# Gathers behind the turned expert, a spread cut into chunks, and an earlier end of the sort: a DeltaNet block with a grouped mixture of experts

## The chip, the cores and the metric

The kernel runs on one core of a Trainium2 chip. TensorE (matmuls), VectorE, ScalarE, GpSimd and SyncE work side by side, each through its own queue in order, and wait for each other through semaphores; sixteen DMA engines move the data. The metric is the device time of one execution in microseconds (us).

## The reference

Two blocks follow each other. The first is a DeltaNet attention over 4 batches, 8 heads, 768 positions and 48 features per head; the keys are normalised first:

```
for t in range(S):
    y[:, :, t] = einsum('bhd,bhde->bhe', q[:, :, t], state)
    v_old = einsum('bhde,bhd->bhe', state, kt)
    state = state + bt * einsum('bhd,bhe->bhde', kt, vt - v_old)
```

Its output, laid out as 3072 tokens of 384 features, is the input x of the second block. That is a mixture of 16 experts in 4 groups. A token takes the group with the largest logit, then the expert with the largest logit inside this group; its result is the product of both softmax weights with `relu(x @ w1) @ w2` of that expert (384 to 1024 to 384).

## The kernel before

**Attention.** The sequence is cut into 24 chunks of 32 positions; one chunk of all batches and heads is a period of the loop over `u` (L672). Four chunks form a group (`RG = 4`). For each group `inverse(g)` (L268) builds on VectorE the inverse of 32x32 triangular matrices, 256 of them at a time, in some 90 dependent steps; its result is turned into `mt` (L372, one buffer) and then spread into `mtb` (L378): for each parity `a`, ScalarE copies `mt` times a mask of the parity. Before the change the first chunk's rows of both parities are spread first (two copies of 128x256), and the other three chunks' rows follow in one copy of 128x768 for each parity. `advance(u)` (L403) runs the recurrence: `a_ps` (L415), its copy `f` (L419), `w_ps` from `mtb` and `f` (L432), its copy `w` (L435), the state `s_ps` (L442) and its two copies into `s_bd` (L448), and the output `o_ps`, copied to `x` (L465). `mask` (L263) and `scale` (L396) prepare operands for it on VectorE. `gram` (L229) makes the products for a chunk ten periods ahead. `logits(u)` (L475) turns a finished chunk, copies it to `xt` (L486) and makes the router's logits.

**The order** is written out by hand: long tasks (`inverse`, `route`) are generators that are pushed forward between the recurrence's steps, either by `work(n)`, which hands out a share of VectorE's time, or by `allow(X)`, which releases a task held at the name X (`ACT_STEP`, `PE_STEP`, `SORT`, `NEXT`, ...). Each engine's queue follows this order.

**Routing.** `route(r)` (L495) takes the logits of a group of chunks: groups 0 to 4 hold four chunks each, 5 and 6 hold two each. It finds each token's expert and place in the expert's list. For `early` groups part of this runs on GpSimd and yields for whole periods; otherwise all of it is on VectorE. For each chunk a 128x256 matrix `at` (L583, two buffers) is compared out, and four matmul instructions sort the chunk's token numbers into `s_sort` (L590). `found` is the copy of the sorted lists (L734); `by_place` (L130) writes the lists of source rows, target rows and gates.

**Experts.** They run in order of their loads, with 224, 232, 220, ... 168 slots (`SLOTS`), the first one expert 0 fixed. For each: `hidden` (L833) makes `h_ps` with three PSUM buffers and `hid` by a ReLU on ScalarE (L842); `second` (L852) makes `y_ps` in three blocks with two buffers and copies them to `yt` (L860). In fp32 each matmul stands as two instructions, so each of the two products is 48 of them. The result is turned (`part_out`, L891), passed through DRAM, weighed (L905) and scattered by GpSimd (L867). Weights are loaded two experts ahead (L163, L170) by SyncE. The rows of experts 2 to 15 are gathered in quarters: `take_quarters` (L807) issues 6 or 7 indirect DMAs (L811) on GpSimd into `xq` (two buffers), and `cross_in` (L817) turns them into `xt` (L819). At the start of expert `e`, `fetch(e + 2)` calls the gathers; `cross_in(e + 1)` stands behind the first block of `second` of expert `e`, and VectorE reaches it directly behind `part_out(e - 1)`. GpSimd's order in this stage is the planner's, the other engines' is the program's.

The rows of experts 0 and 1 are gathered whole and turned by `turn_in` (L799), through PSUM tile `t_ps` with one buffer.

Of the kernel before, what the change touches and what calls it, by code (L numbers as in the profile page):

```python
# [8 lines left out]
F32 = mybir.dt.float32  # L9
I32 = mybir.dt.int32  # L10
AX = mybir.AxisListType
ALU = mybir.AluOpType
ACT = mybir.ActivationFunctionType
# [3 lines left out]
RG = 4  # L17
SHARE = 0.64
LEAD = 10
FIXED, TILE = 1, 128  # L20
LAST = 8
SLOTS = [224] * FIXED + [232, 220, 214, 208, 204, 202, 200, 198, 194, 190, 186, 184, 180, 174, 168]
ACT_STEP, PE_STEP, SOON, NEXT, TURN = "ScalarE", "TensorE", "end of the period", "next period", "its turn"
SORT, ROOTS, FACTOR = "sorting", "roots made", "factor made"


# [39 lines left out]
def deltanet_then_moe(  # L66
# [107 lines left out]
    with ExitStack() as first:  # L174
# [93 lines left out]
        def inverse(g):  # L268
# [105 lines left out]
            yield C * C  # L374
            turned_over.add(g)

            def spread(rows, a):
                nc.scalar.activation(mtb[:, rows, a], mt.rearrange("p i r -> p r i")[:, rows], ACT.Copy,  # L378
                                     scale=cut["parity"][:, a:a + 1])

            rest = slice(0, RG * H)
            yield ACT_STEP
            for a in range(2):
                spread(slice(0, H), a)
            mts[g] = mtb
            rest = slice(H, RG * H)
            for a in range(2):
                yield ACT_STEP
                spread(rest, a)
            mts[g] = mtb  # L390

        def scale(u):

# [101 lines left out]
        def route(r):  # L495
# [8 lines left out]
                               bufs=3)[:, 0:n]  # L504

            L5 = 1 + G
            early = n == RG
            lg = lg_.pop(r)[:, 0:n].rearrange("p n (s e) -> p n s e", s=L5)
            best, hot5, tie = small("best", [L5]), small("hot5", [L5, EG]), small("tie", [L5])
            sx = small("sx", [L5, EG])  # L510
# [68 lines left out]
            else:  # L579
                yield 128  # L580
            for g, u in enumerate(us):
                at = wk.tile([128, T, TILE], F32, tag="at", name=f"at{u}")
                (nc.gpsimd if early else nc.vector).tensor_scalar(  # L583
                    at.rearrange("p t i -> p (t i)"), cut["places"], place[:, u:u + 1], None,
                    op0=ALU.is_equal)
                if r < NGR - 2 and u == u0:
                    yield NEXT
                yield SORT
                for t in range(T):
                    nc.tensor.matmul(s_sort[:, t * 3 * NE:(t + 1) * 3 * NE], lhsT=at[:, t],  # L590
                                     rhs=mine[:, g].rearrange("p c e -> p (c e)"),
                                     start=False, stop=True, skip_group_check=True)
# [42 lines left out]
        with tc.manual_schedule(engines={mybir.EngineType.PE, mybir.EngineType.DVE,  # L635
                                         mybir.EngineType.Activation, mybir.EngineType.Pool,
                                         mybir.EngineType.SP}):
            nc.scalar.activation(rooted, cut["tiny"], ACT.Exp)
            homes = [None, s_ps[:, 0:2], s_ps[:, 2:4]]
            first_grams = ([(u, (0,)) for u in range(RG)] + [(u, (0, 1)) for u in range(RG, 2 * RG)]  # L640
                           + [(u, (1,)) for u in range(RG)])
            for i, (u, parts) in enumerate(first_grams):
                gram(u, homes[i % len(homes)], parts)
                for late, loads in bursts.get(i, ()):
                    nc.scalar.activation(late[:, 0:1], cut["tiny"], ACT.Copy)
                    for load in loads:
                        load()
            start(inverse(0), 1)
            work(22)
            for _ in range(6):  # L650
                work(12)
            scale(0)
            nc.gpsimd.memset(acc[:, 0], 0.0)
            nc.gpsimd.tensor_copy(what[:, :, 0:2], cut["ids"].rearrange("p (u c) -> p u c", c=2))
            ahead = advance(0)
            next(ahead)
            for u in range(2 * RG, LEAD):
                gram(u, homes[u % len(homes)])
            start(inverse(1), 0.95)
            made = 0  # L660
            while 0 not in mts:
                work(4)
                if 1 not in vhs and 0 in turned_over:
                    mask(0)
                    scale(1)
                allow(ACT_STEP)
                made += 1
                if made == LAST:
                    allow(ROOTS)
            allow(FACTOR)  # L670
            ahead_of = {u: [u + LEAD] if u + LEAD < NCH else [] for u in range(NCH + 1)}
            for u in range(NCH + 1):  # L672
                step = advance(u) if u < NCH else iter([None] * 4)
                turned = logits(u - 1) if u else iter([None] * 2)
                if u:
                    next(step)
                else:
                    step = ahead
                allow(FACTOR)
                allow(NEXT)  # L680
                allow(TURN)
                r = group_of.get(u - 2)
                if r is not None and group_of.get(u - 1) != r and r < NGR - 2:
                    start(route(r), 0.25)
                next(turned)
                work(10)
                allow(SORT)
                next(step)
                for v in ahead_of[u]:
                    gram(v)  # L690
                if ahead_of[u]:
                    next(step)
                    next(turned)
                else:
                    next(turned)
                allow(PE_STEP)
                allow(ACT_STEP)
                work(9)
                if not ahead_of[u]:
                    next(step)  # L700
                next(step)
                work(14)
                allow(ACT_STEP)
                allow(ROOTS)
                r = group_of.get(u - 1)
                if r is not None and group_of.get(u) != r and r >= NGR - 2:
                    start(route(r), 0.6 if r == NGR - 2 else 1)
                allow(SOON)
                if u % RG == RG - 3 and u // RG + 2 < NGR:
                    start(inverse(u // RG + 2), SHARE)  # L710
                work(12)
                if u + 1 < NCH:
                    mask(u + 1)
                if u + 2 < NCH:
                    scale(u + 2)
                if u + NB < NCH:
                    load_kq(u + NB)
                if u + NV < NCH:
                    load_kv(u + NV)
                if u < NCH:  # L720
                    nc.sync.dma_start(out=x_dram[u * 128:(u + 1) * 128], in_=xs[u])
                if pieces and u + LEAD >= NCH:
                    pieces.pop(0)()
            while behind:
                work(2)
                allow(PE_STEP)
                allow(ACT_STEP)
                allow(SOON)
                allow(NEXT)
                allow(SORT)  # L730

            n_ps = ps.tile([128, NE], F32, tag="s", name="n_ps")
            nc.tensor.matmul(n_ps, lhsT=ones, rhs=acc[:, NCH], start=True, stop=True)
            nc.vector.tensor_copy(found.rearrange("p t c e -> p (t c e)"), s_sort)  # L734
            by_place(found[:, :, :, 0:FIXED], slice(0, FIXED))
            nc.vector.tensor_copy(last, n_ps)


            key, rank = cp.tile([128, NE], F32, name="key"), cp.tile([128, NE], F32, name="rank")
            nc.vector.scalar_tensor_tensor(key, in0=last, scalar=16.0, in1=cut["tie"], op0=ALU.mult,  # L740
                                           op1=ALU.add)
            like = [128, NE, NE]
            nc.vector.tensor_tensor(table, key[:, None, :].to_broadcast(like),
                                    key[:, :, None].to_broadcast(like), op=ALU.is_gt)
            nc.vector.tensor_reduce(rank, table, axis=AX.X, op=ALU.add)
            nc.vector.tensor_tensor(table, rank[:, None, :].to_broadcast(like),
                                    cut["expert"][:, :, None].to_broadcast(like), op=ALU.is_equal)
# [48 lines left out]
                in_offset=bass.IndirectOffsetOnAxis(ap=rows[0:P, t:t + 1], axis=0))  # L796
        return xg

    def turn_in(xg, xt, i, P):  # L799

        t_ps = ps.tile([128, DC, P], F32, tag="t", name="t_ps", bufs=1)
        for j in range(DC):
            nc.tensor.transpose(out=t_ps[:, j], in_=xg[0:P, i, j * 128:(j + 1) * 128],
                                identity=ident[0:P, 0:P])
# [1 line left out]

    def take_quarters(rows, R):  # L807

        xq = mp.tile([128, T * TILE // BL, DB], F32, tag="xq", name="xq", bufs=2)
        for g in range(-(-R // BL)):  # L810
            nc.gpsimd.indirect_dma_start(  # L811
                out=xq[:, g, :], out_offset=None,
# [118 lines left out]
    with tc.manual_schedule(engines={mybir.EngineType.PE, mybir.EngineType.DVE, mybir.EngineType.SP,  # L931
                                     mybir.EngineType.Activation}):
        for i in range(T):
            turn_in(ready[0], xts[0], i, tiles_of[0][i])
        placed = sort_experts(mp)
        for e in range(FIXED, 2):
            load(e, fetch(e))
# [137 lines left out]
```

## Time and profile before

| what | value |
|---|---|
| median of 3 runs | 545.43 us (545.0 to 546.75) |
| the profiled execution's own time | 545.04 us |
| its span, first to last instruction | 543.1 us |
| TensorE busy | 475.2 us (87%) |
| VectorE busy | 243.7 us (45%) |
| GpSimd busy | 201.7 us (37%) |
| ScalarE busy | 185.6 us (34%) |
| mean granted TensorE clock | 0.963 |

Busy shares are means over two very different stages: the attention until about 231 us, and the experts from 247 us on. A granted clock of 1.00 stands for the upper of TensorE's two levels, 0.50 for the lower. Matmul rows show when TensorE's queue handed them out, with modelled ends; when their result was seen shows in the row of the engine that waited for them. GpSimd's spans are rough.

### The profile page before, as it was taken

The numbers are of one execution on the slowest core, as the hardware profiler recorded it, in microseconds if no ns is written. First come the engines' busy times: TensorE is split into PE (matmuls) and PEld (weight loads), VectorE is DVE, ScalarE is ACT, GpSimd is POOL, SyncE is SP. The second block draws the span as 40 slices with busy tenths as digits, with TensorE's granted clock in tenths as the row PEclk, the third lists the DMA queues.
The fourth block names the chain that finished last, engine by engine and source line by source line (L and its number), as shares of the span: only waits on it lengthen the run. The fifth ranks groups of instructions, "written<-read, shape, count | busy, mean of one in ns | idle before, by whom it ended". The sixth has DMA issues, their size and how long they took to land.

```text
span 543.1 us, 18129 instructions
## 1 busy us (share of the span) xinstructions
PE 475.2 (87%) x7814; PEld 437.7 (81%) x7814; DVE 243.7 (45%) x800; ACT 185.6 (34%) x381; POOL 201.7 (37%) x305
## 2 busy tenths in 40 slices
PE   3348999999999999958943999999999999999993
PEld 3336877888887788848932999899999999999993
DVE  3999999999999952255110101110111111011110
ACT  3226576765857666411001111111111111121220
POOL 0040302627246143231572155345555445451131
PEclk9999999999999999976985999999999999999997
DMA  5771535444315543015852586776899788888720
GB/s 169 268 254 53 167 138 159 145 145 149 113 67 162 160 153 110 33 32 141 273 181 59 179 275 207 260 219 214 287 301 288 245 271 289 254 270 292 274 84 21
DMA packets 57331, 99.94 MB, mean 184 GB/s; under 512 B 18973, under 2 KB 41431, under 8 KB 57249
## 3 DMA queue, kind: packets, MB, share of 16 engines
q1 hardware_dynamic: 51329, 88.76, 50.4%
q0 software_dynamic: 5920, 10.00, 6.1%
q8 instruction: 63, 1.03, 0.8%
q14 instruction: 19, 0.16, 0.1%
HBM read 84.61 MB, written 14.27 MB: 182 GB/s over the span
## 4 chain that ended last, share of the span: by engine, by line
PE 59%; ACT 12%; DMA 10%; DVE 5%; issue 5%; another core or an unknown queue 4%; SPq 3%; POOL 1%; ACTq 0%; POOLq 0%; DVEq 0%
PE h_ps L839 17%; PE y_ps L858 16%; DMA out_dram<-yo,to_i 5%; ACT s_bd L448 5%; PE w_ps L432 5%; ACT mtb L378 4%; PE s_ps L442 4%; PE l_ps L490 2%; PE g_ps L246 2%; PE o_ps L424 2%; PE a_ps L415 2%; DMA yr<-y_dram 2%; SPq L899 2%; PE s_ps L590 2%
## 5 line engine op out<-in xcount | busy, mean ns | idle before, releaser
L839 PE MATMUL h_ps<-xt,w 128*128 128x224 f32 (+15 forms) x768 | 137.6, 339 | 17.0 <-ACT hid L842 12.8
L839 PEld LDWEIGHTS h_ps<-xt,w 128*128 128x128 f32 x768 | 132.7, 195 | 19.5 <-ACT hid L842 13.8
L858 PE MATMUL y_ps<-hid,w 128*128 128x224 f32 (+15 forms) x768 | 133.0, 332 | 2.5 <-ACT yt L860 2.5
L858 PEld LDWEIGHTS y_ps<-hid,w 128*128 128x128 f32 x768 | 128.8, 190 | 3.7 <-ACT yt L860 3.5
L811 POOL DMA_INDIRECT xq<-x_dram,from_q x92 | 87.7, 954 | 40.0 <-issue 25.6
L905 DVE TENSOR_SCALAR yo<-yr,gate 128x384 f32<-128x384 f32 (+14 forms) x28 | 11.2, 418 | 169.8 <-DMA yr<-y_dram 139.7
L842 ACT ACTIVATE hid<-h_ps 128x448 f32<-128x448 f32 (+15 forms) x64 | 31.9, 502 | 129.1 <-PE h_ps L839 95.8
L867 POOL DMA_INDIRECT out_dram<-yo,to_i x32 | 34.0, 1062 | 85.1 <-DVE yo L905 69.9
L860 ACT ACTIVATE yt<-y_ps 128x224 f32<-128x224 f32 (+15 forms) x48 | 15.8, 336 | 120.4 <-PE y_ps L858 103.6
L355 DVE TENSOR_TENSOR t<-m 128x81 f32<-128x81 f32 (+13 forms) x156 | 51.7, 331 | 0.2
L361 DVE TENSOR_TENSOR m<-m,t 128x81 f32<-128x81 f32 (+13 forms) x156 | 51.7, 332 | 0.0
L448 ACT ACTIVATE s_bd<-s_ps 48x768 f32<-48x768 f32 x46 | 37.0, 804 | 10.4 <-PE s_ps L442 9.8
L338 DVE SCALAR_TENSOR_TENSOR m<-m 128x29 f32<-128x29 f32 (+27 forms) x174 | 40.2, 234 | 0.4
L891 DVE STREAM_TRANSPOSE yq<-yt 128x672 f32<-128x672 f32 (+2 forms) x14 | 11.9, 853 | 51.3 <-ACT yt L860 51.3
L432 PE MATMUL w_ps<-f,mtb 64*64 64x48 f32 x768 | 28.0, 224 | 3.8 <-ACT mtb L378 2.9
L583 POOL TENSOR_SCALAR at<-con,place 128x256 f32<-128x256 f32 x20 | 20.5, 1029 | 28.0 <-PE s_ps L590 27.8
L246 PE MATMUL g_ps<-kqt 48*32 48x64 f32 (+1 forms) x1216 | 18.1, 240 | 14.3 <-issue 9.6
L432 PEld LDWEIGHTS w_ps<-f,mtb 64*64 64x64 f32 x768 | 25.0, 138 | 6.5 <-ACT mtb L378 3.2
L415 PEld LDWEIGHTS a_ps<-s_bd,kqt 128*32 128x32 f32 x736 | 15.3, 111 | 16.3 <-ACT s_bd L448 8.2
L378 ACT ACTIVATE mtb<-mt,con 128x256 f32<-128x256 f32 (+1 forms) x24 | 28.2, 1202 | 0.7 <-DVE mt L372 0.6
L529 POOL TENSOR_TENSOR acc<-acc,hots 128x16 f32<-128x16 f32 x20 | 7.2, 361 | 55.2 <-DVE hots L527 54.0
L246 PEld LDWEIGHTS g_ps<-kqt 48*32 48x32 f32 x1216 | 14.5, 118 | 16.2 <-issue 10.9
(141 smaller groups left out, 572.9 us busy)
## 6 DMA issues: line engine op xcount, KB each, us to landing
w<-in_w_dram SPq DMA_DIRECT2D x29, 1536.0 KB
kv<-in_kv_dram SPq DMA_DIRECT2D x24, 448.0 KB
kqt<-in_kq_dram SPq DMA_DIRECT2D x20, 512.0 KB
x_dram<-x SPq DMA_DIRECT2D x24, 192.0 KB
w<-in_w_dram SPq DMA_DIRECT2D x24, 128.0 KB
y_dram<-yq SPq DMA_DIRECT2D x36, 84.0 KB
yr<-y_dram SPq DMA_DIRECT2D x14, 192.0 KB
kqt<-in_kq_dram SPq DMA_DIRECT2D x8, 256.0 KB
```

The costliest lines, as they stand in the source:

```text
L246: nc.tensor.matmul(g_out[quads[b], hh * NP + j, of], lhsT=kqt[rows, 0, j, quads[b]], rhs=kqt[rows, of, j, quads[b]], start=True, stop=True ...
L338: nc.vector.scalar_tensor_tensor(row, in0=m[:, j, 0:j], scalar=m[:, i, j:j + 1], in1=row, op0=ALU.mult, op1=ALU.add)
L355: nc.vector.tensor_tensor(tv, m[:, j + 2:, j:j + 1].to_broadcast([128, n, j]), m[:, j:j + 1, 0:j].to_broadcast([128, n, j]), op=ALU.mult)
L361: nc.vector.tensor_tensor(below, below, tv, op=ALU.add)
L378: nc.scalar.activation(mtb[:, rows, a], mt.rearrange("p i r -> p r i")[:, rows], ACT.Copy, scale=cut["parity"][:, a:a + 1])
L432: nc.tensor.matmul(w_ps[b, h], lhsT=mt[b, uu * H + (h % 2) * NP + h // 2], rhs=f[b, h], start=True, stop=True, skip_group_check=True)
L448: nc.scalar.activation(s_bd[rows, :, :, hh, :], s_at[rows, :, :, hh * D:(hh + 1) * D], ACT.Copy)
L811: nc.gpsimd.indirect_dma_start(out=xq[:, g, :], out_offset=None, in_=x_dram[:, :].rearrange("n (q c) -> (n q) c", q=4), in_offset=bass.Ind ...
L839: nc.tensor.matmul(h_ps[:, k], lhsT=w1[:, j, (f + k) * 128:(f + k + 1) * 128], rhs=xt[:, j, 0:R], start=(j == 0), stop=(j == DC - 1), skip ...
L842: nc.scalar.activation(hid[:, f:f + 2], h_ps, ACT.Relu)
L858: nc.tensor.matmul(y_ps, lhsT=w2[:, f, j * 128:(j + 1) * 128], rhs=hid[:, f], start=(f == 0), stop=(f == FC - 1))
L867: put = nc.gpsimd.indirect_dma_start(out=out[:, :], out_offset=bass.IndirectOffsetOnAxis(ap=to[0:P, i:i + 1], axis=0), in_=yo[0:P, :], in_ ...
```

## The change

1. `xq` has one buffer instead of two. A gather for the next expert then has to wait for the `cross_in` that reads the expert in front.
2. The spread of `mt` is eight copies of 128x256, a pair for each chunk, instead of two of 128x256 and two of 128x768. The first pair stays where it was; the other three pairs are released by a new name `SPREAD`, one copy behind `f` and one behind `xt` in each of the periods 1, 2, ... The very first copy is moved to VectorE.
3. Group 4 of the routing (the last one of four chunks) no longer counts as `early`, so that VectorE does its work; `at` has four buffers instead of two; `SORT` is allowed a second time in the last periods.
4. The lists of expert 0 are written from the PSUM sums directly, ahead of the copy to `found`, and the two turns of its rows go through two PSUM tiles.

```diff
+SPREAD = "spread"
...
-            def spread(rows, a):
-                nc.scalar.activation(mtb[:, rows, a], mt.rearrange("p i r -> p r i")[:, rows], ACT.Copy,
-                                     scale=cut["parity"][:, a:a + 1])
-
-            rest = slice(0, RG * H)
+            def spread(uu, a):
+                rows = slice(uu * H, (uu + 1) * H)
+                from_, by = mt.rearrange("p i r -> p r i")[:, rows], cut["parity"][:, a:a + 1]
+                if g == uu == a == 0:
+                    nc.vector.tensor_scalar(mtb[:, rows, a], from_, by, None, op0=ALU.mult)
+                else:
+                    nc.scalar.activation(mtb[:, rows, a], from_, ACT.Copy, scale=by)
+
             yield ACT_STEP
             for a in range(2):
-                spread(slice(0, H), a)
+                spread(0, a)
             mts[g] = mtb
-            rest = slice(H, RG * H)
-            for a in range(2):
-                yield ACT_STEP
-                spread(rest, a)
-            mts[g] = mtb
+            for uu in range(1, RG):
+                for a in range(2):
+                    yield SPREAD
+                    spread(uu, a)
...
-            early = n == RG
+            early = r < NGR - 2
...
-                at = wk.tile([128, T, TILE], F32, tag="at", name=f"at{u}")
+                at = wk.tile([128, T, TILE], F32, tag="at", name=f"at{u}", bufs=4)
...
+                if u:
+                    allow(SPREAD)
                 r = group_of.get(u - 2)
                 if r is not None and group_of.get(u - 1) != r and r < NGR - 2:
                     start(route(r), 0.25)
                 next(turned)
+                if u:
+                    allow(SPREAD)
...
                 allow(PE_STEP)
                 allow(ACT_STEP)
+                if u == 0:
+                    for _ in range(2):
+                        allow(SPREAD)
+                if u + 2 >= NCH:
+                    allow(SORT)
...
+            by_place(s_sort.rearrange("p (t c e) -> p t c e", t=T, c=3)[:, :, :, 0:FIXED],
+                     slice(0, FIXED))
             nc.vector.tensor_copy(found.rearrange("p t c e -> p (t c e)"), s_sort)
-            by_place(found[:, :, :, 0:FIXED], slice(0, FIXED))
...
-    def turn_in(xg, xt, i, P):
+    def turn_in(xg, xt, i, P, tag="t"):
-        t_ps = ps.tile([128, DC, P], F32, tag="t", name="t_ps", bufs=1)
+        t_ps = ps.tile([128, DC, P], F32, tag=tag, name="t_ps", bufs=1 if tag == "t" else None)
...
-        xq = mp.tile([128, T * TILE // BL, DB], F32, tag="xq", name="xq", bufs=2)
+        xq = mp.tile([128, T * TILE // BL, DB], F32, tag="xq", name="xq", bufs=1)
...
-            turn_in(ready[0], xts[0], i, tiles_of[0][i])
+            turn_in(ready[0], xts[0], i, tiles_of[0][i], "to"[i])
```

## Rows read from the trace of the kernel before

**Rows 1.** The page: shares of the chain that ended last, by engine

```profile
PE 59%; ACT 12%; DMA 10%; DVE 5%; issue 5%; another core or an unknown queue 4%; SPq 3%; POOL 1%; ACTq 0%; POOLq 0%; DVEq 0%
```

**Rows 2.** Stretches: length, busy us of PE, PEld, DVE, ACT, POOL, granted clock, DMA

```profile
40.00:195.70 155.70, 148.16 (x4318) 124.78 (x4320) 152.84 (x546) 103.67 (x188) 53.45 (x118) 1.00 0.41 132
...
247.40:259.70 12.30, 12.30 (x51) 11.75 (x51) 6.39 (x17) 1.63 (x3) 2.07 (x2) 0.75 0.73 172
...
270.30:298.80 28.50, 12.03 (x51) 10.36 (x50) 2.43 (x4) 1.82 (x5) 15.13 (x17) 0.70 0.39 117
...
396.50:526.50 130.00, 130.00 (x825) 129.95 (x824) 19.39 (x34) 25.09 (x60) 55.43 (x63) 1.00 0.79 262
```

**Rows 3.** Timeline of TensorE's matmuls: start, length, line, shapes, idle before

```profile
267.11 3.21 PE L858 MATMUL y_ps<-hid,w 128*128 128x224 f32 x16
270.15 6.63 PE L839 MATMUL h_ps<-xt,w 128*128 128x232 f32 x33
...
294.51 4.24 PE L839 MATMUL h_ps<-xt,w 128*128 128x232 f32 x12 [12.76 <-ACT hid L842]
...
307.99 9.08 PE L839 MATMUL h_ps<-xt,w 128*128 128x220 f32 x48
316.91 6.11 PE L858 MATMUL y_ps<-hid,w 128*128 128x220 f32 x32
323.99 3.24 PE L858 MATMUL y_ps<-hid,w 128*128 128x220 f32 x16 [0.97 <-ACT yt L860]
```

**Rows 4.** Timeline of ScalarE beside them

```profile
275.55 0.36 ACT L860 ACTIVATE yt<-y_ps 128x224 f32<-128x224 f32 x1 [8.15 <-PE h_ps L839]
293.90 1.46 ACT L842 ACTIVATE hid<-h_ps 128x464 f32<-128x464 f32 x3 [18.00 <-remote]
...
323.58 0.60 ACT L860 ACTIVATE yt<-y_ps 128x220 f32<-128x220 f32 x2 [5.93 <-PE y_ps L858]
```

**Rows 5.** Timeline of GpSimd: two unbroken runs of indirect DMAs, first and last

```profile
261.27 0.95 POOL L811 DMA_INDIRECT xq<-x_dram,from_q  x1 [6.83 <-DVE from_q L830]
...
286.33 0.94 POOL L811 DMA_INDIRECT xq<-x_dram,from_q  x1 [0.30 <-issue]
...
289.40 0.97 POOL L867 DMA_INDIRECT out_dram<-yo,to_i  x1 [0.30 <-issue]
...
310.67 1.00 POOL L811 DMA_INDIRECT xq<-x_dram,from_q  x1 [0.85 <-DVE xt L819]
...
318.24 0.94 POOL L811 DMA_INDIRECT xq<-x_dram,from_q  x1 [0.30 <-issue]
...
321.60 1.04 POOL L867 DMA_INDIRECT out_dram<-yo,to_i  x1 [0.31 <-issue]
```

**Rows 6.** Timeline of VectorE: expert 2's rows are turned

```profile
276.74 0.84 DVE L819 STREAM_TRANSPOSE xt<-xq 128x672 f32<-128x672 f32 x1
```

**Rows 7.** Stretches from one copy `w` to the next, columns as in the second group

```profile
102.58:111.22 8.64, 8.22 (x253) 6.87 (x257) 8.57 (x35) 7.10 (x12) 3.65 (x4) 1.00 0.51 169
...
119.86:127.78 7.92, 7.92 (x252) 6.85 (x257) 7.88 (x32) 4.51 (x9) 4.37 (x14) 1.00 0.48 165
```

**Rows 8.** ScalarE's groups by shape: the spread, count, busy us, mean ns

```profile
L378 ACT ACTIVATE mtb<-mt,con 128x768 f32<-128x768 f32 x12 | 19.9, 1662 | 0.0
...
L378 ACT ACTIVATE mtb<-mt,con 128x256 f32<-128x256 f32 x12 | 8.3, 741 | 0.6 <-DVE mt L372 0.6
```

**Rows 9.** Timeline around the last group's inverse

```profile
194.47 1.25 DVE L372 STREAM_TRANSPOSE mt<-m 128x1024 f32<-128x1024 f32 x1
...
199.57 1.35 ACT L378 ACTIVATE mtb<-mt,con 128x256 f32<-128x256 f32 x2
```

**Rows 10.** Timeline between attention and experts

```profile
240.18 0.26 DVE L734 COPY found<-s_ps 128x96 f32<-128x96 f32 x1 [1.28 <-PE s_ps L590]
...
246.11 0.74 PE L803 MATMUL t_ps<-con,xg 96*128 96x96 f32 x3 [0.65 <-DVE xt L805]
```

## The prediction

> **What bounds the kernel now.** I read first the chain that ended last, then stretches of the span, then timelines of the stretches that stood out. The chain goes to TensorE for 59% [rows 1], but as a mean over two stages. By stretches, the late experts are bound by TensorE alone: busy 130.0 of 130.0 us at full clock [rows 2]. There only fewer matmul instructions could help, and the change takes none away. In the attention TensorE is busy 148.16 of 155.70 us and VectorE 152.84 [rows 2]: both are nearly full, so a gain on one is soon capped by the other. What sticks out is the stretch of expert 1: TensorE busy 12.03 of 28.50 us [rows 2].
>
> In its timeline the second product of expert 0 is handed out until 267.11 + 3.21 = 270.32, and `hidden` of expert 1 starts, fills its three PSUM buffers, and stops at 276.78 [rows 3]. ScalarE is what should empty them. It reads the third block of `y_ps` at 275.55, though the matmuls were handed out 5.2 us before, and its first `hid` stands at 293.90, behind 18.00 us that end with something the trace can't name [rows 4]. TensorE resumes in full only at 294.51 [rows 3]. GpSimd issues indirect DMAs in one unbroken run from 261.27 to 290.37, 23 of them, 21 being gathers of experts 2, 3 and 4 [rows 5]. Two buffers let experts 2 and 3 go at once, and `cross_in` of expert 2 at 276.74 [rows 6] frees the buffer for expert 4 before the run is through. The stall ends 3.5 us after the run does.
>
> One stage later is the counterexample. A run of 9 (7 gathers, 2 scatters) lasts from 310.67 to 322.64 [rows 5]. `hidden` of expert 2, beside it, takes 9.08 us for 48 instructions without an idle time, so ScalarE was on time. Only the first two blocks of `second` were seen late, at 323.58, and that cost TensorE 0.97 us [rows 3, 4]. My reading: while GpSimd issues indirect DMAs without a break, signals from TensorE to ScalarE come through for about the first 9 us, and after that only when the run is over. With 9 in a row nearly nothing is lost, with 23 nearly all that lies behind the first nine.
>
> **One buffer for the gathers.** The instructions stay the same; a wait is added in front of each expert's gathers. The first run is then expert 2's 7 gathers alone, 7 x 1.25 = 8.8 us by the spacing (310.67 to 318.24 is six steps, 1.26 each [rows 5]), so 261.3 to about 270. Expert 3's have to wait for `cross_in` of expert 2, which VectorE reaches near the start of `hidden` of expert 1: some 2 to 4 us of pause. The next run is 7 gathers and 2 scatters, which has the length of the good one. So `hidden` of expert 1 should go at the pace of expert 2's: 9.08 x 232/220 = 9.58 us. It was done at 294.51 + 4.24 = 298.75 [rows 3]. Gone are 298.75 - 270.32 - 9.58 = 18.85 us. Against this I set one lateness as at 323.99, 1.0. **Net 17.9.** The bounds: if the pause doesn't clear what the first run delayed, 3 to 12 us of the stall remain (3.5 is how long it took to clear at 290.37; 12 is a run of 16 in place of 23: (16 - 7) x 1.3); at best all 18.85 go.
>
> Behind the added wait on GpSimd stand the scatters and the rest of its queue. For these nothing on TensorE's path waits soon: an expert's gathers have until its own `cross_in`, one expert's time further on. A late expert has two products of some 7.5 us, about 15 us in all, and its gathers take 6 x 1.26 = 7.6 us to issue, leaving about 7 for landing. I price this at 0 in the forecast; its cover being gone is the last rival.
>
> **The spread.** The two copies of 128x768 cost ScalarE 1.66 us each, those of 128x256 0.74 [rows 8]; the six new ones take 4.4 us a group in place of 3.3. A period with the long copy lasts 8.64 us, the period behind the spread 7.92 [rows 7]: 0.72 us for each of two periods. ScalarE's copies `f` and `x` stand behind the long ones, and TensorE's next step behind those. For groups 1 to 3 this makes six times 0.72, **4.3 us**; the other groups I count at nothing, the least sure part of this term. A short copy of 0.74 lies in the time in which ScalarE waits for TensorE anyway; where it doesn't fit whole I allow 0.05 for each of 18 pairs, 0.9 in all. So 3.4, from 1 (pairs that cost 0.2) to 5 (all groups gain). The cap is VectorE: the last group's `mt` is turned at 194.47 + 1.25 = 195.72 and read at 199.57 [rows 9], a lead of 3.85 us. TensorE can catch up no more than this, less some 0.4 for the copy put on VectorE. Both give **3.3**. That first copy on VectorE runs beside ScalarE's second one of the pair: nothing by itself.
>
> **Sort and start of the experts.** More buffers for `at` and the earlier `SORT` move matmul instructions of the sort ahead; their number stays. The lists written before `found` spare its 0.26 us on the way to the first gathers; the second PSUM tile spares the turn 0.65 us of waiting [rows 10], of which I take 0.4, since the copy behind it still has to be made. The sort's end I take at 0.25 gained, against 0.4 for the work put into full periods (group 4's routing on VectorE). **Net 0.5**, from -1 to +1.5.
>
> **The clock.** From 247.4 to 259.7 TensorE's granted level is 0.75 in the mean [rows 2], so half of these 12.3 us at the lower level: the first expert starts slow, after a transition in which TensorE did little. If the work starts 3.8 us earlier but the rise stays where it is, 3.8 us more of it run at half speed: 1.9 lost. If the rise moves with the work, 0. **I take 0.9**, the middle, since no row shows which.
>
> Sum: 17.9 + 3.3 + 0.5 - 0.9 = 20.8. From the profiled time of 545.04, which is 0.4 below the median shown, **524.3 us**.
>
> **Rivals.**
>
> *A part of the stall stays.* For: I don't know what the signals wait on, and a lateness could carry over from a run of 7 to one of 9 behind a pause of only 2 to 4 us, when clearing took 3.5 us in both rows. Against: 9 in a row did almost no harm. Remaining 3 to 12 us give 528 to 536.
>
> *The stall stays whole, the gathers being not its cause.* For: the first 18.00 us wait is put down to no engine, and the stretch is also one where the weights of expert 2 are loaded. Against: the DMA share there, 0.39, is half that of the late experts, 0.79, which have no such stall [rows 2]. Time: 545.04 - 3.3 - 0.5 + 0.9, about 542. The Trainium skill ("SBUF — State Buffer", section "SBUF: two separate sides") says that engines and DMAs reach SBUF by disjoint ports, so that neither slows the other. By that rule gathers would leave ScalarE alone and the time would be this rival's. The trace agrees with it in that `hidden` of expert 2 is undisturbed beside a run; it disagrees if the late blocks at 323.58 hang on that run.
>
> *No change that can be told:* the stall stays and the attention's gain is used up by VectorE: within 0.3%, 1.6 us, which is about what a measurement of this kernel can tell from none.
>
> *Slower: gathers come too late.* With one buffer, expert e+2's gathers can't start before expert e+1 is turned; a scatter put ahead of them in the planner's order holds them further, because in-order GpSimd waits for the scatter's data, which is ready 14.65 us behind the start of `hidden` (322.64 - 307.99, to the scatter's end [rows 3, 5]). Then 14.65 + 7.6 = 22 us are needed where a late expert lasts 15. The landing has the turn before it too. Every us beyond the cover costs a us for each of some 13 experts, so from 20.8/13 = 1.6 us beyond, the kernel is slower than before: at 3 us beyond, 524.3 + 39 = 563. Against: in the rows of before the gathers lie ahead of the scatters in the run [rows 5], and the start of expert e+2's gathers lies some two experts' products ahead of their use. The Trainium skill ("Trainium Kernel Development and Optimization", section "Best Practices") advises double buffers to overlap transfers with work, which speaks for this rival; no run here shows one buffer yet.
>
> **How the numbers follow.** The stall gone: 0.62, between 518 and 528 (its bounds: 18.85 + 5 + 1.5 = 25.4, to 519.7, with a us or so for gains counted at nothing; and 17.9 + 1 - 1 - 1 = 16.9, to 528). Partly gone: 0.18, 528 to 538, with the attention's lower bound. Stall whole: 0.10, 542, still faster by 0.55%. No change: 0.04. Slower: 0.06. The likeliest is 524.3. The range 518 to 538 holds the first two, 0.80. Faster 0.62 + 0.18 + 0.10 = 0.90, same 0.04, slower 0.06.
>
> **What would show it.** Right: GpSimd's first run of gathers is 7 long, with a pause before the next; `hidden` of expert 1 takes about 9.6 us with no idle time of TensorE behind `hid`; the periods behind each inverse last about 7.9 in place of 8.64; the last `mt` is read within 1 us of being made. Wrong: ScalarE's `hid` of expert 1 still late though the run is short (the partial or whole rival); idle time of TensorE behind `xt` of a late expert, with VectorE's turn waiting on a gather (the slower rival); copies `f` or `xt` put off by the short spreads, so that all periods, not two in four, are longer; a half-level clock that lasts longer into expert 0.

## The result, and the profile after

The changed kernel takes **522.4 us** (median of 4, 521.55 to 524.41), the kernel before beside it 545.21: a ratio of 0.9585, 95% interval 0.9549 to 0.9622. The forecast was 524.3, from 518 to 538. The profiled execution of the changed kernel took 524.41, the longest of the four; its mean granted clock is 0.974, that of the others 0.978 to 0.981.

The chain of the changed kernel by engine, to be held against [rows 1], and its stretches, with the columns of [rows 2]: the attention, three periods behind an inverse as in [rows 7], the end of the attention in two parts, the first product of expert 0, and both products of expert 1.

```profile
PE 67%; DMA 12%; DVE 6%; ACT 5%; issue 4%; POOL 2%; another core or an unknown queue 1%; SPq 1%; DVEq 0%; POOLq 0%; ACTq 0%
```

```profile
40.00:195.70 155.70, 150.57 (x4391) 127.43 (x4393) 153.41 (x545) 107.59 (x207) 54.13 (x119) 1.00 0.42 134
101.98:110.43 8.45, 8.20 (x253) 6.85 (x258) 8.38 (x34) 6.99 (x13) 3.73 (x5) 1.00 0.50 159
110.43:118.74 8.31, 8.18 (x253) 6.95 (x258) 8.28 (x33) 5.75 (x11) 0.00 (x0) 1.00 0.46 149
118.74:126.67 7.93, 7.93 (x253) 6.86 (x258) 7.93 (x32) 5.76 (x12) 3.87 (x12) 1.00 0.46 148
...
222.60:229.40 6.80, 6.21 (x182) 5.51 (x181) 1.24 (x9) 3.20 (x9) 0.00 (x0) 1.00 0.09 31
229.40:236.00 6.60, 4.97 (x21) 4.60 (x21) 2.52 (x15) 1.13 (x5) 0.00 (x0) 0.50 0.09 32
246.15:257.30 11.15, 11.15 (x50) 10.83 (x51) 6.42 (x17) 1.63 (x3) 2.07 (x2) 0.83 0.72 181
267.70:287.60 19.90, 19.09 (x98) 18.20 (x97) 2.44 (x4) 3.20 (x7) 8.70 (x10) 1.00 0.72 229
```

In the last row TensorE is busy 19.09 of 19.90 us. From `hidden` of expert 1 to `hidden` of expert 2 it now takes 19.88 us in place of 37.84. The timelines of TensorE, ScalarE and GpSimd, as in [rows 3 to 5]:

```profile
246.15 11.17 PE L852 MATMUL h_ps<-xt,w 128*128 128x224 f32 x48 [0.55 <-DVE xt L818]
...
267.75 9.56 PE L852 MATMUL h_ps<-xt,w 128*128 128x232 f32 x48
277.15 6.43 PE L871 MATMUL y_ps<-hid,w 128*128 128x232 f32 x32
284.40 3.40 PE L871 MATMUL y_ps<-hid,w 128*128 128x232 f32 x16 [0.81 <-ACT yt L873]
287.63 9.08 PE L852 MATMUL h_ps<-xt,w 128*128 128x220 f32 x48
```

```profile
270.31 0.56 ACT L855 ACTIVATE hid<-h_ps 128x464 f32<-128x464 f32 x1 [1.11 <-PE h_ps L852]
...
283.98 0.62 ACT L873 ACTIVATE yt<-y_ps 128x232 f32<-128x232 f32 x2 [6.07 <-PE y_ps L871]
```

```profile
258.88 0.94 POOL L824 DMA_INDIRECT xq<-x_dram,from_q  x1 [5.67 <-DVE from_q L843]
...
266.36 0.95 POOL L824 DMA_INDIRECT xq<-x_dram,from_q  x1 [0.30 <-issue]
...
271.16 0.95 POOL L824 DMA_INDIRECT xq<-x_dram,from_q  x1 [0.88 <-DVE xt L832]
...
281.85 0.95 POOL L880 DMA_INDIRECT out_dram<-yo,to_i  x1 [0.30 <-issue]
```

The first run is 7 gathers and ends at 267.31; a pause of 3.85 us follows, then 7 gathers and 2 scatters. `hidden` of expert 1 takes 9.56 us, its first `hid` comes at 270.31, and the one lateness left in this expert leaves TensorE idle for 0.81 us before 284.40.

Both traces side by side, each step as the start of the same instruction group in the changed kernel less that in the kernel before (the span falls from 543.15 to 522.50, 20.65 in all):

| step | from | gained, us | forecast |
|---|---|---|---|
| to `a_ps` of period 22 | 217.75, now 214.53 | 3.22 | 3.3 (spread) |
| from there to `n_ps` | 239.94, now 239.11 | -2.39 | sort: 0.5 in all with the next row |
| to `hidden` of expert 0 | 247.40, now 246.15 | 0.42 | |
| to `hidden` of expert 1 | 270.15, now 267.75 | 1.15 | -0.9 (clock) |
| to `hidden` of expert 2 | 307.99, now 287.63 | 17.96 | 17.9 (stall) |
| to the end | | 0.29 | 0 |

### The profile page after: what moved, and what is told of

Read it like the earlier page. It is cut to its first block, busy times and chain, and to the rows that moved or that the text cites. A ratio compares the mean times of both kernels' runs of the same rounds, so it can differ in the third digit from the quotient of the medians.

```text
span 522.5 us, 18175 instructions
## 1 busy us (share of the span) xinstructions
PE 473.5 (91%) x7814; PEld 437.3 (84%) x7814; DVE 246.3 (47%) x815; ACT 190.4 (36%) x404; POOL 193.8 (37%) x288
## 4 chain that ended last, share of the span: by engine, by line
PE 67%; DMA 12%; DVE 6%; ACT 5%; issue 4%; POOL 2%; another core or an unknown queue 1%; SPq 1%; DVEq 0%; POOLq 0%; ACTq 0%
PE h_ps L852 18%; PE y_ps L871 17%; DMA out_dram<-yo,to_i 5%; PE w_ps L435 5%; PE s_ps L445 5%; PE l_ps L493 3%; PE a_ps L418 3%; ACT s_bd L451 3%; DMA y_dram<-yq 3%; PE o_ps L459 3%; PE o_ps L427 3%; PE g_ps L247 2%; PE a_ps L412 2%; PE t_ps L485 2%; PE s_ps L593 2%
## 5 line engine op out<-in xcount | busy, mean ns | idle before, releaser
L852 PE MATMUL h_ps<-xt,w 128*128 128x224 f32 (+15 forms) x768 | 133.9, 334 | 0.6 <-DVE xt L818 0.6
L852 PEld LDWEIGHTS h_ps<-xt,w 128*128 128x128 f32 x768 | 130.6, 192 | 1.4 <-DVE xt L818 0.8
L824 POOL DMA_INDIRECT xq<-x_dram,from_q x92 | 87.6, 952 | 37.8 <-issue 23.9
L451 ACT ACTIVATE s_bd<-s_ps 48x768 f32<-48x768 f32 x46 | 37.0, 804 | 13.7 <-PE s_ps L445 13.1
L384 ACT ACTIVATE mtb<-mt,con 128x256 f32<-128x256 f32 x47 | 34.3, 743 | 0.9 <-DVE mt L373 0.9
L247 PE MATMUL g_ps<-kqt 48*32 48x64 f32 (+1 forms) x1216 | 18.6, 240 | 14.8 <-issue 9.0
L445 PE MATMUL s_ps<-w,kv 32*128 32x96 f32 x736 | 27.6, 287 | 0.1
L532 POOL TENSOR_TENSOR acc<-acc,hots 128x16 f32<-128x16 f32 x16 | 5.3, 330 | 60.1 <-DVE hots L530 59.1
```

The costliest lines, as they stand in the source:

```text
L247: nc.tensor.matmul(g_out[quads[b], hh * NP + j, of], lhsT=kqt[rows, 0, j, quads[b]], rhs=kqt[rows, of, j, quads[b]], start=True, stop=True ...
L384: nc.scalar.activation(mtb[:, rows, a], from_, ACT.Copy, scale=by)
L445: nc.tensor.matmul(s_at[:, b, j], lhsT=k[quads[b], j], rhs=w[quads[b], 2 * j:2 * j + 2], start=(u == 0 and j == 0), stop=True, skip_group_ ...
L451: nc.scalar.activation(s_bd[rows, :, :, hh, :], s_at[rows, :, :, hh * D:(hh + 1) * D], ACT.Copy)
L824: nc.gpsimd.indirect_dma_start(out=xq[:, g, :], out_offset=None, in_=x_dram[:, :].rearrange("n (q c) -> (n q) c", q=4), in_offset=bass.Ind ...
L852: nc.tensor.matmul(h_ps[:, k], lhsT=w1[:, j, (f + k) * 128:(f + k + 1) * 128], rhs=xt[:, j, 0:R], start=(j == 0), stop=(j == DC - 1), skip ...
```

## The experiments

**One buffer and nothing else**, on the kernel before.

```
-        xq = mp.tile([128, T * TILE // BL, DB], F32, tag="xq", name="xq", bufs=2)
+        xq = mp.tile([128, T * TILE // BL, DB], F32, tag="xq", name="xq", bufs=1)
```

> The kernel before with one buffer for the gathers and nothing else of the change. Run theory (a long unbroken run of indirect DMAs holds TensorE's signals to ScalarE back): the first run is 7 gathers, hidden of expert 1 takes about 9.6 us, and the time falls by 17 to 19 us, to 526 to 528. Rival, that the gathers do not cause the stall (or only with the other edits): hidden of expert 1 still takes over 20 us and the time stays at 544 to 546. Rival, that one buffer makes late gathers: idle time of TensorE behind xt of late experts.

Measured: 527.66 (526.07 to 529.3) against 545.06, ratio 0.9689, interval 0.9652 to 0.9727. TensorE's timeline:

```profile
271.14 9.56 PE L839 MATMUL h_ps<-xt,w 128*128 128x232 f32 x48
280.54 9.72 PE L858 MATMUL y_ps<-hid,w 128*128 128x232 f32 x48
```

The buffer alone is worth 17.4 us, and late gathers are not seen: of all the `hidden`, only expert 0's waits for `xt`, 0.55 us, as before.

**All but the buffer**, on the changed kernel.

```
-        xq = ... bufs=1)
+        xq = ... bufs=2)
```

> The changed kernel with two buffers again; all else of the change stays. Run theory: 21 gathers in a row, hidden of expert 1 takes about 28 us, the time is 522.4 + 18 = 540 to 541. If spread, sort and lists had cured the stall, it stays at 522 to 523.

Measured: 542.42 (540.76 to 545.41), ratio to before 0.9958, interval 0.9935 to 0.9981; that is 20.0 us above the changed kernel, 1.4 above the expected range. The stall is back, as ScalarE's and TensorE's timelines show:

```profile
289.25 1.46 ACT L855 ACTIVATE hid<-h_ps 128x464 f32<-128x464 f32 x3 [17.93 <-remote]
```

```profile
289.86 5.01 PE L852 MATMUL h_ps<-xt,w 128*128 128x232 f32 x12 [12.73 <-ACT hid L855]
```

So spread, sort and lists have no part in curing it; together they are worth 0.2% to 0.65%. The buffer alone was worth 17.4 us on the kernel before and is worth 20.0 here; why these differ isn't shown.

**The spread alone**: part 2 of the change on the kernel before.

> The kernel before with the spread cut into chunks (first copy on VectorE) and nothing else. My term of 3.3 us: the copy f of period 22 is some 3.2 us earlier, and if that lead lives to the end the time is 542 (0.994). Rival, that the lead is given back between attention and experts (the tail of the routing and the lower clock): earlier by 3 us in period 22, but the time at 543.5 to 545.

Measured: median 541.85 of ten (535.38 to 544.69) against 545.06, 3.2 us less; the ratio, 0.9907 with an interval of 0.9874 to 0.994, is lower than that of the medians, 0.994, as it leans on the one execution of 535.38. In the trace `a_ps` of period 22 starts at 214.92 in place of 217.75, and `hidden` of expert 0 at 244.54 in place of 247.40: 2.8 us won in the attention, and here they live to the start of the experts. By the median the first reading holds. The execution that was traced took 543.62, though, 1.4 less than the 545.04 of the kernel before: its stall is 0.9 us longer, and a late expert is 2.1 us longer than there.

**Without the third part**: group 4 early again, two buffers for `at`, no second `SORT`, on the changed kernel.

> The changed kernel without its third part: group 4 early again, two buffers for at, no second SORT. From the traces, the added sort instructions take 1.1 to 1.4 us in periods 21 and 22 and the lower clock begins 7 us earlier. If that is a loss: 520 to 521.5, faster than the changed kernel by 1 to 2. Rival, that the sort has to be done anyway and stands at the end instead: 522.5 to 523.5.

Measured: 523.01 (521.85 to 523.18). That can't be told from 522.4, and the first reading, 520 to 521.5, did not come. Yet in its trace `hidden` of expert 0 starts at 243.50, 2.65 us ahead of the changed kernel's: period 22 lasts 7.12 us in place of 8.48 there, and the lower clock comes later, as stretches show (columns as above):

```profile
229.40:232.90 3.50, 1.84 (x17) 1.74 (x17) 2.25 (x12) 0.51 (x3) 0.59 (x1) 1.00 0.01 3
232.95:239.50 6.55, 3.54 (x17) 3.27 (x16) 3.56 (x17) 0.00 (x0) 3.05 (x4) 0.50 0.00 0
```

The lead has grown to 3.9 us by `hidden` of expert 10, and 2.3 of it are lost in this one expert, where two scatters stand directly in front of six gathers. GpSimd's, ScalarE's and TensorE's timelines:

```profile
419.93 1.03 POOL L878 DMA_INDIRECT out_dram<-yo,to_i  x1 [5.84 <-DVE yo L916]
...
428.93 0.95 POOL L822 DMA_INDIRECT xq<-x_dram,from_q  x1 [0.31 <-issue]
```

```profile
431.45 0.49 ACT L853 ACTIVATE hid<-h_ps 128x380 f32<-128x380 f32 x1 [4.88 <-remote]
```

```profile
431.99 6.07 PE L869 MATMUL y_ps<-hid,w 128*128 128x190 f32 x36 [2.07 <-ACT hid L853]
```

A run of 8 lasts 9.95 us and leaves TensorE idle for 2.07 us: the same effect in small.

**Longer runs on purpose.** Four variants of the changed kernel add work on GpSimd behind expert 2's seven gathers, into a tile that nobody reads:

```
             ready[e] = take_quarters(from_q[:, e], SLOTS[e])
+            if e == 2:
+                for k in range(7):       # 14 in the second; dq[0:16] in the third
+                    nc.gpsimd.indirect_dma_start(out=dq[0:128, k, :], ...)
...
+                for k in range(14):      # the fourth
+                    nc.gpsimd.tensor_copy(dq, con[:, 0:512])
```

> The changed kernel, where expert 2's 7 gathers are followed at once by 7 more of the same rows into a tile that nobody reads: an unbroken run of 14, which ends near 276.4 in place of 267.3. Run theory: TensorE's signals that are due after about 9 us of the run (268) are seen 1 to 3.5 us behind its end, so hidden of expert 1 stops at about 274.4 and goes on at 277.5 to 280: 3 to 5.5 us lost there. Rival, that one buffer cures the stall in another way than by the length of the run (the wait itself, or fewer transfers under way at once): hidden stays at 9.6 us.

> The same with 14 more gathers: a run of 21, that ends near 285.2. Run theory: hidden of expert 1 goes on at 286 to 288.7, so it lasts about 24 us and 12 to 14.5 us are lost; the loss grows by as much as the run does, 8.75 us more than with a run of 14. Rival: no loss, or one that doesn't grow with the run.

> The same with 7 more gathers, but each of 16 rows in place of 128, an eighth of the bytes and of the descriptors. If the instruction and GpSimd's time for it count: the run is as long as with 14 whole ones and 3 to 5.5 us are lost. If what counts is the number of rows under way: the run theory in its simple form is wrong, and nothing or under 1 us is lost.

> The changed kernel, where expert 2's 7 gathers are followed by 14 GpSimd copies of 128x512 (0.61 us each) and no extra gather; GpSimd's order in the experts' stage is that of the program. GpSimd is as long without a break as in the run of 14. If indirect DMAs hold the signals back: hidden of expert 1 takes 9.6 us and its hid are on time. If GpSimd's being busy does it: 3 to 5.5 us lost, as with 14 gathers.

Measured, one execution each: 519.63, 522.18, 519.74 and 520.18. It looked as if the theory fell: with 14 more gathers, and expert 3's behind them without a pause, GpSimd issues 30 indirect DMAs in a row and TensorE loses nothing.

```profile
259.18 0.94 POOL L824 DMA_INDIRECT xq<-x_dram,from_q  x1 [6.07 <-DVE from_q L843]
...
295.53 0.95 POOL L880 DMA_INDIRECT out_dram<-yo,to_i  x1 [0.30 <-issue]
```

```profile
268.06 9.56 PE L852 MATMUL h_ps<-xt,w 128*128 128x232 f32 x48
277.46 9.56 PE L871 MATMUL y_ps<-hid,w 128*128 128x232 f32 x48
286.86 9.08 PE L852 MATMUL h_ps<-xt,w 128*128 128x220 f32 x48
```

But the kernel before, run on that same chip, took 522.33, not 545. All four ran on a chip on which there is next to nothing to lose, so they say nothing of what the stall depends on elsewhere, the fourth one included. They do show what is left without any lateness: an expert's two products follow each other at 18.80 us (286.86 - 268.06) where the changed kernel's profile has 19.88.

**A pause instead of one buffer**: the kernel before, two buffers, on another chip. Experts 3 and 4 copy the tile in front into their own before they gather, so they start when it has landed.

```
+        if behind is not None:
+            nc.gpsimd.tensor_copy(xq[:, 0:n], behind[:, 0:n])
...
+            ready[e] = take_quarters(from_q[:, e], SLOTS[e], ready[e - 1] if e in (3, 4) else None)
```

> The kernel before, two buffers kept; experts 3 and 4 start their gathers only when those of the expert in front have landed (a GpSimd copy from the one tile to the other stands between). Run theory: a break of 4 to 5 us after 7 gathers is enough, hidden of expert 1 takes about 9.6 us, and the time is that of one buffer alone, 526 to 529. Rival, that one buffer works by something else than the break: the stall of about 18 us stays, 543 to 546.

Measured: 538.38 (536.83 to 538.92) against 544.29, ratio 0.9877, interval 0.9833 to 0.9921. Neither reading as it stood. Expert 1 is cured (48 instructions in 9.56 us), but the gathers of expert 5 now follow those of expert 4 without a pause, and the stall is one expert later. GpSimd's and ScalarE's timelines:

```profile
285.99 0.98 POOL L814 DMA_INDIRECT xq<-x_dram,from_q  x1 [0.27 <-POOL xq L812]
...
307.70 1.04 POOL L870 DMA_INDIRECT out_dram<-yo,to_i  x1 [0.30 <-issue]
```

```profile
297.35 0.54 ACT L845 ACTIVATE hid<-h_ps 128x440 f32<-128x440 f32 x1 [4.70 <-PE h_ps L842]
311.39 0.97 ACT L845 ACTIVATE hid<-h_ps 128x440 f32<-128x440 f32 x2 [13.50 <-remote]
```

One run of 18 is left, and the wait ends 2.6 us behind it.

**Another engine waits**: the four ReLU copies of expert 1 on VectorE, in the kernel before.

```
+            if R == SLOTS[1]:
+                nc.vector.tensor_scalar(hid[:, f:f + 2], h_ps, 0.0, None, op0=ALU.max)
```

> The kernel before, with the four ReLU copies of expert 1 on VectorE in place of ScalarE. If TensorE's signals come late whoever waits for them: VectorE reads h_ps at 290 to 294 too, and hidden of expert 1 still takes about 28 us. If it is ScalarE that is held up: hidden takes 9.6 to 12 us, and ScalarE's y copies alone are late.

Measured: 544.31. VectorE's first copy is late too, behind a wait of 13.30 us (ScalarE's was 18.00), and comes 2.6 us after the end of a run (279.45 + 0.95). It comes at 283.00 and not at the expected 290 to 294, since the run is shorter:

```profile
263.19 0.94 POOL L811 DMA_INDIRECT xq<-x_dram,from_q  x1 [6.57 <-DVE from_q L830]
...
279.45 0.94 POOL L811 DMA_INDIRECT xq<-x_dram,from_q  x1 [0.30 <-issue]
```

```profile
283.00 0.64 DVE L843 TENSOR_SCALAR hid<-h_ps 128x464 f32<-128x464 f32 x1 [13.30 <-remote]
```

So it is not ScalarE that is held up; what comes from TensorE is late for either reader. At least in part it is the signal and not the product: in the kernel before, ScalarE's three `hid` at 293.90 follow each other in 1.46 us [rows 4], where blocks take some 2.4 us each without a stall (9.56 for four), so the first block was done almost 4 us before it was seen, or more. Whether the products were late as well isn't shown. What ScalarE tells VectorE does come through: in the kernel before, 14.7 us into the run, VectorE starts as soon as ScalarE's copy at 275.55 [rows 4] is through.

```profile
275.94 0.88 DVE L891 STREAM_TRANSPOSE yq<-yt 128x672 f32<-128x672 f32 x1 [8.15 <-ACT yt L860]
```

With VectorE's copies the expert lasts 26.2 us in place of 37.8 because `cross_in`, now queued behind these copies on VectorE, releases expert 4's gathers later and so cuts the run to 14. A second long run, of 16 (290.44 to 310.28), follows and takes the rest: expert 2 lasts 28.5 us in place of 19.1.

**A pause in the middle, and a long run of small gathers**: two variants of the changed kernel, on a chip where the kernel before takes 543.21.

```
         for g in range(-(-R // BL)):
+            for _ in range(pause if g == 4 else 0):
+                nc.gpsimd.tensor_copy(idle, con[:, 0:512])
...
+            ready[e] = take_quarters(from_q[:, e], SLOTS[e], 5 if e < 8 else 0)
```

> The changed kernel with five GpSimd copies of 128x512 (0.67 us each) between the fourth and the fifth gather of experts 2 to 7; GpSimd's order in the experts' stage is that of the program. On a chip on which the kernel before takes 545: by the run theory runs are now 5 us long, nothing is due 9 us into one, and the lateness left in the changed kernel (about 3.4 us over experts 1 to 9) falls to under 1: 519 to 520.5. If GpSimd's work of any kind keeps a run going: as the changed kernel or slower, 522 to 526. On a chip on which the kernel before takes 522: no change that can be told from the changed kernel's time there.

> The changed kernel with 14 more gathers of 16 rows each behind expert 2's seven: an unbroken run of 21, to about 285, with a third of the rows. On a chip on which the kernel before takes 545: if the length of the run decides, hidden of expert 1 goes on at 286 to 289 and 12 to 14.5 us are lost, about 535; if the rows under way decide, under 1.5 us is lost, 520 to 524. On a chip on which the kernel before takes 522: nothing lost, as with the run of 21 whole gathers.

The pause: 521.34 (519.88 to 522.92), ratio 0.9602, interval 0.9549 to 0.9654, not to be told from the changed kernel's; the expected 519 to 520.5 did not come. Where the pause stands it does what was expected; GpSimd's and TensorE's timelines:

```profile
280.24 3.32 POOL L825 COPY idle<-con 128x512 f32<-128x512 f32 x5
```

```profile
266.60 9.56 PE L855 MATMUL h_ps<-xt,w 128*128 128x232 f32 x48
276.00 9.56 PE L874 MATMUL y_ps<-hid,w 128*128 128x232 f32 x48
285.40 9.08 PE L855 MATMUL h_ps<-xt,w 128*128 128x220 f32 x48
294.32 9.08 PE L874 MATMUL y_ps<-hid,w 128*128 128x220 f32 x48
303.24 7.04 PE L855 MATMUL h_ps<-xt,w 128*128 128x214 f32 x38
```

No idle time is left, and 18.80 and 17.84 us are the lengths seen on the chip without the stall. GpSimd is at work all through the 3.32 us of copies, so its being busy is not the trouble: its indirect DMAs in a row are. Part of the gain is lost in the late experts, which have no such pause; experts 8 and 10 are 1.77 and 0.95 us longer than on the chip without the stall:

```profile
394.42 2.28 PE L855 MATMUL h_ps<-xt,w 128*128 128x198 f32 x12 [1.50 <-ACT hid L858]
```

The small gathers: 551.77 in one execution, slower than the kernel before by 8.6, though each of the 14 moves an eighth of the rows. An unbroken run of 30 lasts from 258.71 to 294.86:

```profile
300.84 1.46 ACT L855 ACTIVATE hid<-h_ps 128x464 f32<-128x464 f32 x3 [26.92 <-remote]
```

```profile
301.45 4.50 PE L852 MATMUL h_ps<-xt,w 128*128 128x232 f32 x12 [14.78 <-ACT hid L855]
```

I had reckoned with a run of 21 and 12 to 14.5 us; expert 3's gathers and two scatters joined it, because `cross_in` of expert 2 was through before the extra gathers were. The loss is larger than that and goes with the run's length, not with the rows.

On the chips that have the stall, the length of a long run and what it cost stand in line. The cost is the stage's length less the undisturbed one (18.80 for expert 1, 17.84 for expert 2), or the idle time where one is named:

| run | length, us | cost, us | length less cost |
|---|---|---|---|
| without the third part, a late expert | 9.95 | 2.1 (idle) | 7.9 |
| changed kernel, expert 1 (271.16 to 282.80) | 11.6 | 1.1 | 10.5 |
| VectorE's copies, expert 1 | 17.2 | 7.4 | 9.8 |
| VectorE's copies, expert 2 | 19.8 | 10.7 | 9.2 |
| pause instead of one buffer, expert 2 | 22.8 | 13.7 | 9.1 |
| all but the buffer, expert 1 (256.73 to 285.71) | 29.0 | 19.9 | 9.1 |
| kernel before, expert 1 [rows 5] | 29.1 | 19.0 | 10.1 |
| the spread alone, expert 1 (257.00 to 286.32) | 29.3 | 20.0 | 9.4 |
| small gathers, expert 1 | 36.2 | 28.8 | 7.4 |

The first two rows are short runs, and for these the line doesn't hold: in these traces other runs of 10 to 13 us cost between nothing and 2.1 us. In three of the long ones some 2 us of the cost is the lower clock: behind the stall the last 12 matmuls of `hidden` take 4.24 us in the kernel before and 5.01 and 4.50 in the two other runs shown, where a quarter of an undisturbed `hidden` is 2.4; the mean granted level of the kernel before is 0.70 there [rows 2].

## Why the prediction was right, point by point

**The stall.** Forecast 17.9, measured 17.96 in the traces and 17.4 by the buffer alone. The mechanism, a run's first 9 us or so free and the rest lost, holds in the seven runs over 17 us of the table (7.4 to 10.1 us free). The forecast's reading was too simple in one point: it has signals come through again only when the run is over, but its own row at 275.55 [rows 4] lies 14.3 us into the run and 14.8 before its end, and the pause instead of one buffer shows one at 297.35, inside its run. So single signals do come through, several us late. Set against the length of each expert on the chip without the stall, experts 1 to 14 together lose 22.3 us in the trace before and 4.3 in the changed kernel's, 18.0 less. What the forecast did not have is that it belongs to the chip: on the chip of the four longer runs the kernel before takes 522.33, and there the change can be worth 0 to 3 us (an estimate, from one execution each: 522.33, and 519.63 to 522.18 of the four one-buffer kernels, whose added work costs TensorE nothing). The two traces of the comparison less their lateness give 522.7 and 520.1, which agrees. What in a chip makes the difference is open, and so is what between TensorE and its reader is held up; no run shows whether recording the trace has a part in it.

**The rival of a stall that is only partly gone** was priced at 3 to 12 us; 0.81 came, about what the run of nine cost before (0.97 [rows 3]). The pause of 3.85 us was enough. **The rival by which gathers leave ScalarE alone** (542) fell: the changed kernel without its one buffer takes 542.42, and its run of gathers is the only thing put back. The Trainium skill ("SBUF — State Buffer", section "SBUF: two separate sides") is about data paths, and no run here contradicts it there: with 14 of its 30 transfers cut to an eighth of the rows a run still lost 28.8 us, so the bytes don't decide.

**The slower rival**, gathers too late with one buffer, did not show: from 390 to 510 us TensorE is busy 119.51 of 120.00. The Trainium skill's advice of double buffers ("Trainium Kernel Development and Optimization", section "Best Practices") is answered by the measurement: on a chip with the stall one buffer is 3.1% faster than two, as the second one let a run grow.

**The spread.** 3.3 forecast, 3.22 measured, but the working was off in two places that cancelled. I expected two periods a group at 7.92; they last 8.45 and 8.31 in group 2. In this group 7.92 was out of reach, as the row had shown: of the 8.64 us TensorE was busy 8.22 [rows 7], so no more than 0.42 was to be won there. Groups 1 to 3 gave 2.0 (0.48, 0.52, 0.99 by the starts of `w`) in place of 4.3. And groups 4 and 5, counted at nothing, gave 0.57 and 0.53, the start 0.12. VectorE's cap never closed:

```profile
193.60 1.25 DVE L373 STREAM_TRANSPOSE mt<-m 128x1024 f32<-128x1024 f32 x1
```

```profile
196.89 1.36 ACT L384 ACTIVATE mtb<-mt,con 128x256 f32<-128x256 f32 x2
```

The last `mt` is read 2.04 us after it is made; I had said within 1. It is also made 0.87 earlier than [rows 9], which the cap did not allow for.

**The sort: wrong sign in this pair of traces.** +0.5 forecast, -2.39 + 0.42 = -1.97 measured. Of the 2.39, 1.37 are lost in period 22, where sort instructions were added (8.48 us to the next `a_ps` in place of 7.11; I had allowed 0.4 for all of them), the rest in the tail, whose TensorE steps now run at half clock:

```profile
229.58 0.90 PE L485 MATMUL t_ps<-con,x 128*128 128x128 f32 x3 [0.61 <-ACT x L468]
...
231.12 1.47 PE L493 MATMUL l_ps<-wr,xt 128*128 128x20 f32 x6
```

In the kernel before, the same two took 0.55 and 0.82. Of the 0.42, the second PSUM tile gave 0.47, from the first turn to the second 1.05 us in place of 1.52; I had said 0.4. The lists gave nothing, where I had said 0.26: they are written earlier, but the first gather still starts 1.04 us behind the last sort matmul, before 1.07.

**The clock: wrong sign too, in this pair.** -0.9 forecast, +1.15 measured: `hidden` of expert 0 takes 11.17 us in place of 12.32, as the rise to the upper level came 3.6 us earlier, though the work began only 1.25 earlier. What I left out is that the fall before it can move as well: it came at 229.4 in place of 236.4. Both terms together were forecast at -0.4 and came to -0.82, so the sum, 20.8 against 20.65, was right within 0.2 with two wrong parts in it. That is luck. It also holds for these two executions only: by the medians the gain is 22.8, and no trace shows where the other 2 us lie.

Nor are the tail and the clock shown to be the change's doing: other traces of the same code differ by as much. With VectorE's copies, where the attention is that of the kernel before, TensorE's timeline has

```profile
217.46 0.87 PE L415 MATMUL a_ps<-s_bd,kqt 128*32 128x96 f32 x32 [0.16 <-ACT s_bd L448]
...
242.12 0.57 PE L733 MATMUL n_ps<-acc,con 128*128 128x16 f32 x2
```

This is 24.66 us for the step that takes 22.19 in the kernel before and 24.58 in the changed one. Over all traces it is 22.19 to 24.66 with the old sort and 23.17 to 24.58 with the new one, and the lower level starts 6.4 to 12.0 us behind `a_ps` of period 23, early and late with either. What sets that moment isn't shown. From `a_ps` of period 22 to `hidden` of expert 1 it is 52.4 to 54.6 us in four traces of the attention as before and 51.5 to 53.4 in eight of the changed one, no loss that can be told. Only the 1.37 of period 22 and the 0.4 from `n_ps` to `hidden` of expert 0 are in every trace that has the edit.

## What to carry to other kernels

Look at how long GpSimd issues indirect DMAs without a pause, not at how much they move: on the chips here that show it, nearly all that lay beyond the first 7 to 10 us of a long run was lost to the engine that waited for TensorE, ScalarE or VectorE, and a pause of some 3 us, filled with other GpSimd work or not, was enough. On such a chip a second buffer can cost time when all it does is let such a run grow. And a sum that comes out right does not prove its terms: set the two traces side by side at the same instructions, and look at further traces of the same code before a term of 1 or 2 us is put down to a change.

## What the runs showed of the hardware that was not expected

The same two-buffer kernel takes 522.33 us on one chip and 543 to 545 on two others; a run of 28 whole gathers and two scatters cost nothing on the first, a run of 30 of which 14 were small cost 28.8 us on another. And TensorE's clock can fall to the lower level although the engine was busy 6.21 of the 6.80 us before (222.60 to 229.40), while in the kernel before it stayed at the upper level through a stretch with 4.62 of 6.90 and fell only behind it:

```profile
229.40:236.30 6.90, 4.62 (x98) 4.35 (x97) 3.72 (x20) 1.98 (x8) 0.92 (x1) 1.00 0.09 31
```
